# The opening of an attention-and-MLP kernel: four input tiles loaded in halves by two queues, the first keys through a third, two loads of v held back

## The chip, the cores and the metric

The kernel runs on one core of one Trainium2 chip. The metric is the device time of one execution in microseconds (us). The core has five engines that matter here: TensorE (PE in the profile, its weight loads PEld), VectorE (DVE), ScalarE (ACT), GpSimd (POOL) and SyncE (SP). SP, ACT and POOL can each put transfers on a DMA queue of their own. All three queues feed the same 16 DMA engines.

## The reference, cut to what matters

The input x has 2048 rows of 576 values. It is normalised row by row, and two branches work on the result: a sliding-window attention with 32 query heads and 16 key/value heads over the last 512 cached positions, and a gated MLP. All inputs are bf16.

```python
xn = layernorm(x)                                   # 1 x 2048 x 576
q = heads(xn @ wq)                                  # 32 heads of 128
k, v = k_cache[:, :, 1536:], v_cache[:, :, 1536:]   # 16 heads x 512 x 128, each used by 2 query heads
s = merge(softmax(q @ k.T * 128 ** -0.5) @ v) @ wo
h = gelu(layernorm(xn) @ w1)                        # four column groups, shifted by 1, -1, 2, -2 rows
x1 = xn + shifted(h) @ w2
g = silu(x1 + gelu(layernorm(x1) @ w3) @ w4)
out = x + s * g
```

## The kernel before, in words

**Tiling.** The rows of x are worked on in four blocks of 512 (NB = 4), each of four tiles of 128 rows (TB = 4, P = 128). The attention runs over "heads in blocks", u = 0 to 127, 32 for each block. For each u, PE multiplies the block by the head's part of wq (`stage_q`, or L729 for the first two), then takes the scores against the transposed keys kT (`stage_s`, L566), ACT takes the exponential (L569), and PE multiplies by v (`stage_v`, L588). The MLP follows. From about 9 us on, PE is the engine on which everything ends.

**The opening.** Before the first head can start, block 0 of x has to be loaded, normalised and transposed. Its four tiles live in `xn_b[0]`, seen as `x_first`. Tile 0 is loaded in two column halves, one by ACT's queue (L380) and one by SP's (L381). Tiles 1 and 2 are then loaded whole by SP's queue, and tile 3 whole by ACT's queue (all L384). Behind them SP's queue has, in an order written out by hand, the first two heads of keys (`load_k(0, nc.sync, 2, 0, 2)`, 256 KB, L364), then the first quarter of wq in two column halves (L393, L395), the other two heads of keys, v, more of wq, and so on.

`ln1_first` normalises the block. For tiles 0, 1 and 2, DVE takes the statistics (L431, L432), one tile after the other. Tile 3 goes to ACT, which takes its sum and its sum of squares (L435, L436). ACT also takes the square roots: one for tile 0 as soon as its statistics are there (L434), one for tiles 1 to 3 together (L440). DVE takes the reciprocals (L446 for tile 0, L448 for the others) and applies the result to tiles 0, 1 and 2 (L443); the first 256 columns of tile 3 are applied by ACT (L451) and the others by DVE (L454). The operations stand on each engine in the order in which they are written, and the engines wait for each other through semaphores.

PE meanwhile multiplies the identity 48 times (`warm`, L708), then waits for tile 2's statistics (`warm_behind`, L711) and multiplies five times more. Then it transposes: `tr1_first(pss, (0,))` makes five transposes of tile 0 (L470), `keys_first(0, k01)` four transposes of the first head of keys (L484), then come tile 1 (five), tiles 2 and 3 (ten), and `keys_first(1, k01)` with four more of keys. `xT_first` copies the transposed x out of PSUM (DVE three chunks, L478; ACT two, L476), DVE copies the two heads of keys to `kT` (L723), and PE starts the products for heads 0 and 1 (L729).

**POOL's queue.** POOL builds the identity, fills a few areas with constants (L387, L388, L402) and then puts loads on its queue. At step u = 3 of the head loop stands `load_v(2)`, two loads of 128 KB (v for key heads 4 and 5, L370), and behind it `load_wq(2)` (L345), which waits until PE has used the buffer that it overwrites. POOL has nothing to wait for ahead of `load_v(2)`.

`late(ap, fn)` makes POOL copy one element of `ap` to a scratch word (`gate`, L243) and then issue what `fn` issues, so that the transfers do not start before `ap` has been written.

**Near the end of the kernel,** `load_sx(b)` (L1048) loads, for block b, the attention result from DRAM and x again, through SP's queue; blocks 0 and 1 in one load for each of the two, blocks 2 and 3 in two halves.

Of the kernel before, what the change touches and what calls it, by code (L numbers as in the profile page):

```python
# [8 lines left out]
P = 128  # L9
# [22 lines left out]
def kernel(  # L32
# [14 lines left out]
    nc = tc.nc  # L47
# [15 lines left out]
    NB = S // QB  # L63
    TB = QB // P
# [18 lines left out]
    x2 = A_x.rearrange("b s d -> (b s) d")  # L83
# [158 lines left out]
    def late(ap, fn):  # L242
        g = nc.gpsimd.tensor_copy(out=gate[:, :], in_=ap)  # L243
        with tc.issue_after(g.ins):
            fn()
# [8 lines left out]
    def stage(i):  # L254
        return stage_pool.tile([P, DP * TB], BF16, name=f"stage{i % 2}")
# [43 lines left out]
    with ExitStack() as actx:  # L299
# [31 lines left out]
        x_t = {}  # L331
# [27 lines left out]
        def load_k(i, eng=None, step=4, g0=0, g1=4):  # L359
            if g0 == 0:  # L360
                kst_t[i] = stage(i)
            dst = kst_t[i][:, 0:4 * W].rearrange("p (g a) -> p g a", g=4)
            for g in range(g0, g1, step):
                (eng or nc.gpsimd).dma_start(  # L364
                    out=dst[:, g:g + step, :],
                    in_=A_k_cache[0, 4 * i + g:4 * i + g + step, K0:, :].rearrange("g (p kc) d -> p g (kc d)", p=P))

        def load_v(i, eng=None):
            for g in (2 * i, 2 * i + 1):
                (eng or nc.gpsimd).dma_start(out=v_sb[:, g, :, 0:Dh],  # L370
                                             in_=A_v_cache[0, g, K0:, :].rearrange("(p kc) d -> p kc d", p=P))
# [6 lines left out]
        x_first = xn_b[0][:, :, 0:D]  # L378
        hw = D // 2
        nc.scalar.dma_start(out=x_first[:, 0, hw:D], in_=x2[0:P, hw:D])  # L380
        nc.sync.dma_start(out=x_first[:, 0, 0:hw], in_=x2[0:P, 0:hw])  # L381
        for tt in range(TB):
            if tt:
                (nc.sync if tt < TB - 1 else nc.scalar).dma_start(out=x_first[:, tt, :],  # L384
                                                                  in_=x2[tt * P:(tt + 1) * P, :])
            x_t[0].append(x_first[:, tt, :])
        nc.gpsimd.memset(xn_b[0][:, :, D:], 0.0)  # L387
        nc.gpsimd.memset(wr_first[DR:, :], 0.0)  # L388
        with tc.manual_schedule(engines={SP}):
            load_k(0, nc.sync, 2, 0, 2)  # L390
            for m0 in (0, 2 * Dh):
                cols = slice(m0, m0 + 2 * Dh)
                nc.sync.dma_start(out=wq_b[0][:, :, cols],  # L393
                                  in_=A_wq[0:NF * P, cols].rearrange("(kc p) m -> p kc m", p=P))
                nc.sync.dma_start(out=wr_first[0:DR, cols], in_=A_wq[NF * P:D, cols])  # L395
            load_k(0, nc.sync, 2, 2, 4)
            load_v(0, nc.sync)
            load_wq(1, nc.sync)
            load_wr(1, 2, nc.sync)
            load_v(1, nc.sync)  # L400
            load_k(1, nc.sync)
# [7 lines left out]
        xn_t = {}  # L409
# [51 lines left out]
        def x_banks():  # L461
            a, b = (ps_sc.tile([P, 4, QB], BF16, name="ps_x", tag=f"sc{i}") for i in range(2))
            c, d = (ps_po.tile([P, 2, W], BF16, name="ps_x4", tag="po") for _ in range(2))
            return [c[:, 0, :], d[:, 0, :], a[:, 0, :], b[:, 0, :], b[:, 1, :]], a[:, 2:4, :]
# [15 lines left out]
        def keys_first(g, ps):  # L480
            src = kst_t[0]
            for kc in range(KCH):
                c0 = g * W + kc * P
                nc.tensor.transpose(out=ps[:, g, kc * P:(kc + 1) * P], in_=src[:, c0:c0 + P], identity=ident[:, :])  # L484
# [140 lines left out]
        def at(u, fn):  # L625
            fill.setdefault(u, []).append(fn)
# [64 lines left out]
        at(12, lambda: load_k(3))  # L691
        for g in range(Hkv):
            if g % 2 == 0 and g >= 4:
                at(max(2 * g - 8, 3), lambda g=g: load_v(g // 2))
        for j in range(2, NB * 8):
            at(4 * (j - 1) - 1, lambda j=j: load_wq(j))
        for i, u in enumerate((17, 21, 25, 28, 30, 33, 37, 41)):
# [4 lines left out]
        with tc.manual_schedule(engines={SP, POOL, PE, DVE, ACTE}):  # L702
            mv, nb = ln1_first()
            wu = ps_sc.tile([P, QB], FP32, name="warm", tag="sc0")

            def warm(n):
                for _ in range(n):
                    nc.tensor.matmul(wu[:, 0:112], lhsT=ident[:, :], rhs=ident[:, 0:112], start=True, stop=True)  # L708

            def warm_behind(ap):  # L710
                nc.tensor.matmul(wu[:, 0:1], lhsT=ident[:, :], rhs=ap.bitcast(BF16)[:, 1:2], start=True, stop=True)  # L711

            warm(48)
            warm_behind(mv[:, 2, :])
            warm(5)
            pss, k01 = x_banks()
            tr1_first(pss, (0,))
            keys_first(0, k01)
            tr1_first(pss, (1,))
            tr1_first(pss, (2, 3))  # L720
            keys_first(1, k01)
            xT_first(pss)
            nc.vector.tensor_copy(out=kT[:, 0:2, :], in_=k01[:, :, :])  # L723
            e = small.tile([P, 1], FP32, name="nr_e")
            nc.scalar.activation(out=e[:], in_=nb[:], func=ACT.Exp, scale=0.0)
            psq = [ps_pq.tile([P, QB], FP32, name="psq", tag="pq") for _ in range(2)]
            for u, kcs in ((0, (0,)), (1, (0,)), (0, range(1, NDC)), (1, range(1, NDC))):
                for kc in kcs:
                    nc.tensor.matmul(psq[u][:, :], lhsT=wq_main(u, kc), rhs=xT_b[0][:, kc, :],  # L729
                                     start=(kc == 0), stop=(kc == NDC - 1))  # L730
                if NDC - 1 in kcs:
                    qT_t[u] = qT_pool.tile([P, QB], BF16, name="qT")
                    nc.vector.tensor_copy(out=qT_t[u][:, :], in_=psq[u][:, :])
        turn, done = {}, 0
        for u in range(0, U + 1):
            n = 1
            if u in tr_k_at:
                n = 0
            if 12 < u < ln1_at[0] + 3 or u > WO_AT[1] + TB:
                n = 2  # L740
            n = min(n, OT + Hq * sum(u > v + TB for v in WO_AT.values()) - done)
# [6 lines left out]
        with tc.manual_schedule(engines={SP, POOL, PE}):  # L748
            for u in range(0, max(max(fill), max(pe_fill)) + 1):
                atoms = pe_fill.get(u, [])  # L750
                n = len(atoms)
# [44 lines left out]
    with ExitStack() as bctx:  # L796
# [144 lines left out]
        with tc.manual_schedule(engines={SP, POOL, PE, DVE, ACTE}):  # L941
# [6 lines left out]
            for half in range(2):  # L948
                nc.gpsimd.dma_start(out=w1_q[HALVES[half], :, :],
                                    in_=w1_tail.rearrange("p (g s) -> p g s", g=4)[:, :, P:c4])  # L950
# [18 lines left out]
            for k in range(len(ops) + 1):  # L969
                nxt = None  # L970
                if k < len(ops):
                    f, b, p = ops[k]
# [3 lines left out]
                if pend:  # L976
# [3 lines left out]
                    f, b, p = ops[k - 1]  # L980
# [61 lines left out]
        def load_sx(b):  # L1042
            s_b = sx_pool.tile([P, TB, D], BF16, name="s_b")
            x_b = sx_pool.tile([P, TB, D], BF16, name="x_b")
            n = TB if b < 2 else TB // 2
            for t, src in ((s_b, s_dram), (x_b, x2)):
                for t0 in range(0, TB, n):
                    nc.sync.dma_start(out=t[:, t0:t0 + n, :], in_=rows(src, b * TB + t0, n))  # L1048
            sx_t[b] = (s_b, x_b)
# [150 lines left out]
        with tc.manual_schedule(engines={PE, DVE, ACTE}):  # L1200
# [6 lines left out]
            g, j = 2, 0  # L1207
            for d in range(0, ND, 2):
                b = d // NP
# [56 lines left out]
            b = NB - 1  # L1266
# [15 lines left out]
        with tc.manual_schedule(engines={PE, DVE, ACTE, SP}):  # L1282
# [20 lines left out]
            tt = TB - 1  # L1303
# [22 lines left out]
    with tc.If(flag > 0):  # L1326
        nc.gpsimd.dma_start(out=g_dram[(NT - 1) * P:NT * P, :], in_=g_last)
        with ExitStack() as gctx:
# [20 lines left out]
            with tc.For_i(0, NT, 1) as t:  # L1349
# [10 lines left out]
                with tc.For_i(0, Hq, 1) as h:  # L1360
                    g = h // REP
# [6 lines left out]
                                        in_=A_wq[0:NF * P, cols].rearrange("(kc p) m -> p kc m", p=P))  # L1368
# [72 lines left out]
```

## Time and profile before

| | |
|---|---|
| time, median of three runs | 813.63 us (813.28 to 818.35) |
| time of the profiled execution | 814.01 us |
| span of the profiled execution | 812.2 us |
| PE busy | 806.3 us (99%) |
| DVE busy | 464.7 us (57%) |
| ACT busy | 402.2 us (50%) |
| POOL busy | 95.8 us (12%) |
| granted TensorE clock | 1.0 |

The profile is one execution taken by the hardware profiler. The span runs from the first to the last recorded instruction; the execution's own time of 814.01 us is 1.8 us longer. Times in a timeline count from the start of the span. A row of a timeline gives the start, the time for which the group ran, the engine, the line of the kernel, the operation, what it writes and reads, how many there are (x5), and in brackets how long the engine had been idle before it and what released it. The chain of waits is followed backwards from the last instruction, at each step to what released it, so it shows which work set the end. A DMA row gives the issuing queue, the size and the time from issue to landing.

### The profile page before, as it was taken

Reading aid. Unit: us, or ns where it says so; the run is one execution under the profiler, and the core shown is the slowest. Engines: PE = TensorE matmul, PEld = TensorE weight load, DVE = VectorE, ACT = ScalarE, POOL = GpSimd, SP = SyncE. Lnnn points to the kernel's source line nnn. Section 1 sums busy time; section 2 is a strip of 40 time slices with the busy share of each in tenths; the row PEclk is TensorE's granted clock in tenths of the full one; section 3 lists DMA queues with packets and bytes.
Section 4 is the critical chain, followed back from the end, with each engine's and each line's share of the span. In section 5 each row is a group of like instructions: output and inputs, shape, how many; then the busy total and the mean of one; then the engine's idle time right before and its main releaser. Section 6 shows DMA issues by size and latency. Waiting matters only on the chain.

```text
span 812.2 us, 19806 instructions
## 1 busy us (share of the span) xinstructions
PE 806.3 (99%) x8231; PEld 471.1 (58%) x8231; DVE 464.7 (57%) x1398; ACT 402.2 (50%) x503; POOL 95.8 (12%) x162
## 2 busy tenths in 40 slices
PE   8999999999999999999999999999999999999998
PEld 6666666566655666655666556555555555555555
DVE  5978786228963379752477539353246636655413
ACT  7777777237762377742577542033343333334621
POOL 3333210100010000000100301362000000000000
PEclk9999999999999999999999999999999999999999
DMA  9999881109760187520373372499000410220101
GB/s 218 203 168 222 187 173 57 56 27 141 156 151 9 56 137 139 111 53 27 103 126 76 84 93 61 100 324 255 3 2 16 92 45 16 49 89 17 46 15 39
DMA packets 137437, 80.00 MB, mean 99 GB/s; under 512 B 114784, under 2 KB 128384, under 8 KB 137344
## 3 DMA queue, kind: packets, MB, share of 16 engines
q1 hardware_dynamic: 124656, 40.03, 27.5%
q0 software_dynamic: 11296, 37.27, 16.8%
q8 instruction: 65, 1.06, 0.6%
q10 hardware_dynamic: 1392, 1.40, 0.5%
q14 instruction: 28, 0.23, 0.1%
HBM read 45.38 MB, written 6.93 MB: 64 GB/s over the span
## 4 chain that ended last, share of the span: by engine, by line
PE 99%; DMA 0%; DVE 0%; SPq 0%; issue 0%; ACT 0%
PE ph L1077 15%; PE po L588 15%; PE sc L566 14%; PE psq L548 13%; PE sc L269 12%; PE pm L1114 12%; PE pm L1289 4%; PE pm L1077 3%; PE pm L832 2%; PE pswo L269 2%; PE pr L1114 2%; PE ph L832 1%; PE sc L523 1%; PE pr L269 1%; PE pm L269 1%; PE pr L879 1%
## 5 line engine op out<-in xcount | busy, mean ns | idle before, releaser
L569 ACT ACTIVATE pT<-sc 128x1024 bf16<-128x1024 f32 x256 | 250.5, 1023 | 129.5 <-PE sc L566 129.2
L588 PEld LDWEIGHTS <-pT 128*128 128x128 bf16 x2048 | 133.1, 98 | 54.4 <-issue 5.1
L588 PE MATMUL po<-v_sb,pT 128*128 128x129 bf16 x2048 | 154.7, 220 | 0.0
L566 PE MATMUL sc<-qT,kT 128*128 128x512 bf16 x512 | 152.1, 379 | 0.0
L548 PE MATMUL psq<-xT_b,wq_b 128*128 128x512 bf16 x503 | 129.1, 379 | 0.0
L1077 PE MATMUL ph<-xT_b,w_s 64*128 64x512 bf16 x976 | 127.4, 376 | 0.0
L1114 PE MATMUL pm<-w_s,h 64*128 64x512 bf16 x864 | 122.2, 377 | 0.0
L1095 ACT ACTIVATE h<-ph 128x512 bf16<-128x512 f32 x67 | 39.4, 598 | 132.6 <-PE ph L1077 130.4
L269 PE MATMUL sc<-wo_sb,oT 128*128 128x512 bf16 (+1 forms) x768 | 103.9, 286 | 0.0
L1114 PEld LDWEIGHTS <-h 64*128 64x128 bf16 x1728 | 71.0, 94 | 55.0
L269 PEld LDWEIGHTS <-oT 128*128 128x128 bf16 x1024 | 65.2, 98 | 55.2 <-issue 0.5
L592 DVE RECIPROCAL ri_b<-po 128x2 f32<-128x2 f32 x256 | 40.4, 164 | 97.7 <-PE po L588 88.5
L593 DVE TENSOR_TENSOR o<-po,ri_b 128x256 bf16<-128x256 f32 x216 | 89.7, 422 | 4.9
L1114 PE MATMUL pr<-w_s,h 64*128 64x64 bf16 x864 | 90.3, 189 | 0.0
L1077 PEld LDWEIGHTS <-w_s 64*128 64x128 bf16 x1152 | 56.1, 94 | 48.2 <-issue 0.6
L556 DVE TENSOR_TENSOR qT<-psq,rq 128x512 bf16<-128x512 f32 x82 | 56.6, 691 | 35.5 <-PE psq L548 35.1
L1093 DVE COPY hx<-ph 128x512 f32<-128x512 f32 x55 | 38.1, 692 | 60.4 <-PE ph L1077 60.4
L548 PEld LDWEIGHTS <-wq_b 128*128 128x128 bf16 x503 | 46.3, 98 | 42.6
L566 PEld LDWEIGHTS <-kT 128*128 128x128 bf16 x512 | 44.4, 98 | 28.4 <-issue 0.2
L345 POOL DMA_DIRECT2D wq_b<-in_A_wq_dram x30 | 22.6, 754 | 285.1 <-PE psq L548 256.2
L558 DVE CAST qT<-psq 128x512 bf16<-128x512 f32 x44 | 30.2, 686 | 23.2 <-PE psq L523 21.0
L807 DVE TENSOR_SCALAR hx<-ph,ph 1x1 f32<-1x1 f32 x55 | 11.5, 210 | 46.4 <-PE ph L1077 46.4
(178 smaller groups left out, 727.7 us busy)
## 6 DMA issues: line engine op xcount, KB each, us to landing
wq_b<-in_A_wq_dram POOLq DMA_DIRECT2D x30, 512.0 KB, 4.8
wo_sb<-in_A_wo_dram POOLq DMA_DIRECT2D x8, 576.0 KB, 4.7
w_s<-in_B_w_dram POOLq DMA_DIRECT2D x9, 512.0 KB, 6.3
w_s<-in_B_w_dram POOLq DMA_DIRECT2D x10, 288.0 KB, 5.4
w_s<-in_B_w_dram POOLq DMA_DIRECT2D x4, 576.0 KB, 6.1
out_dram<-o SPq DMA_DIRECT2D x15, 144.0 KB, 1.8
oT<-o SPq DMA_TRANSPOSE x108, 3.3
xn_b<-in_A_x_dram POOLq DMA_DIRECT2D x12, 144.0 KB, 2.8
```

The costliest lines, as they stand in the source:

```text
L269: nc.tensor.matmul(ps, lhsT=oT_t[qb * Hq + h][:, tt, :], rhs=wo_sb[:, h, lo:hi], start=(i == 0), stop=(i == Hq - 1))
L548: nc.tensor.matmul(psq[:, :], lhsT=wq_main(u, kc), rhs=xT_b[qb % 2][:, kc, :], start=(kc == 0 and pos != 1), stop=(kc == n - 1 and (plain ...
L556: behind["qT"] = nc.vector.tensor_tensor(out=qT[:, :], in0=psq[:, :], in1=rq_t.pop(u), op=ALU.add)
L566: nc.tensor.matmul(sc[:, j, :], lhsT=kT[:, g, kc * P:(kc + 1) * P], rhs=qT_t[u][:, :], start=True, stop=True)
L569: nc.scalar.activation(out=pT[:], in_=sc[:], func=ACT.Exp, scale=SCALE)
L588: nc.tensor.matmul(po[:, j, :], lhsT=pTs[kc][:, tt * P:(tt + 1) * P], rhs=v_sb[:, g, kc, 0:Dh + 1], start=(kc == 0), stop=(kc == KCH - 1))
L592: nc.vector.reciprocal(out=ri, in_=po[:, :, Dh])
L593: nc.vector.tensor_tensor(out=o[:, t0:t0 + 2, :], in0=po[:, :, 0:Dh], in1=ri.unsqueeze(2).to_broadcast([P, 2, Dh]), op=ALU.mult)
L1077: nc.tensor.matmul(ps[i][:, :], lhsT=lhsT, rhs=xT[half, kc, :], start=first, stop=last, skip_group_check=True)
L1093: nc.vector.tensor_copy(out=src[:, :], in_=ps[i][:, :])
L1095: nc.scalar.activation(out=h3[:, :], in_=src[:, :], func=ACT.Gelu_apprx_tanh)
L1114: nc.tensor.matmul(out, lhsT=h3_t[b, fc][half, tt * P:(tt + 1) * P], rhs=w4_s[fc // WS][half, fc % WS, lo:hi], start=key not in started, s ...
```

## The change

Five things are changed.

1. Tiles 1, 2 and 3 of x's first block are no longer loaded whole. Each is loaded in two halves of 64 rows, the upper rows by SP's queue and the lower by ACT's, in the order 1, 3, 2.
2. The first two heads of keys go through POOL's queue; they stood on SP's queue behind x. They are issued outside the part of the program whose order is fixed by hand.
3. PE's transposes of the first head of keys move from behind tile 0 to behind tiles 2 and 3, where those of the second head were.
4. `load_v(2)` at step u = 3 stands behind a `late` gate on the first element of tile 0 of the normalised x.
5. `load_sx(2)` loads block 2 whole; only block 3 is still in halves.

```diff
-        for tt in range(TB):
-            if tt:
-                (nc.sync if tt < TB - 1 else nc.scalar).dma_start(out=x_first[:, tt, :],
-                                                                  in_=x2[tt * P:(tt + 1) * P, :])
-            x_t[0].append(x_first[:, tt, :])
+        for tt in (1, TB - 1, 2):
+            for eng, half in ((nc.scalar, 1), (nc.sync, 0)):
+                r0 = half * P // 2
+                eng.dma_start(out=x_first[r0:r0 + P // 2, tt, :], in_=x2[tt * P + r0:tt * P + r0 + P // 2, :])
+        x_t[0] = [x_first[:, tt, :] for tt in range(TB)]
         nc.gpsimd.memset(xn_b[0][:, :, D:], 0.0)
         nc.gpsimd.memset(wr_first[DR:, :], 0.0)
+        load_k(0, nc.gpsimd, 2, 0, 2)
         with tc.manual_schedule(engines={SP}):
-            load_k(0, nc.sync, 2, 0, 2)
             for m0 in (0, 2 * Dh):
...
-                at(max(2 * g - 8, 3), lambda g=g: load_v(g // 2))
+                at(max(2 * g - 8, 3), lambda g=g: load_v(g // 2) if g > 4 else
+                   late(xn_t[0][0:1, 0, 0:1], lambda: load_v(2)))
...
             tr1_first(pss, (0,))
-            keys_first(0, k01)
             tr1_first(pss, (1,))
             tr1_first(pss, (2, 3))
-            keys_first(1, k01)
+            for g in range(2):
+                keys_first(g, k01)
             xT_first(pss)
...
-            n = TB if b < 2 else TB // 2
+            n = TB if b < NB - 1 else TB // 2
```

## The prediction

> **What bounds the kernel now.** I read the page first: the busy times and the chain of waits over the whole span.
>
> ```profile
> span 812.2 us, 19806 instructions
> ...
> PE 806.3 (99%) x8231; PEld 471.1 (58%) x8231; DVE 464.7 (57%) x1398; ACT 402.2 (50%) x503; POOL 95.8 (12%) x162
> ...
> PE 99%; DMA 0%; DVE 0%; SPq 0%; issue 0%; ACT 0%
> PE ph L1077 15%; PE po L588 15%; PE sc L566 14%; PE psq L548 13%; PE sc L269 12%; PE pm L1114 12%; PE pm L1289 4%; PE pm L1077 3%; PE pm L832 2%; PE pswo L269 2%; PE pr L1114 2%; PE ph L832 1%; PE sc L523 1%; PE pr L269 1%; PE pm L269 1%; PE pr L879 1%
> ```
>
> PE is the chain for 99% of 812.2 us, and nothing in the change takes a multiplication away. So the change can only move the time at which PE begins its unbroken work. I therefore read the chain of waits of the first 16 us.
>
> ```profile
> 1.44 3.37 DMA xn_b<-in_A_x_dram
> ...
> 4.83 0.83 DVE ln_st L431 x2
> ...
> 9.10 0.22 PE ps_x L484 x4
> 9.32 2.19 PE psq L729 x10
> ```
>
> The opening is a load (until 4.81), DVE work on it, and PE's transposes; from 9.3 us the chain stays on PE. All that can be won lies ahead of 9.3 us. The timeline of this stretch, in order of time, carries all terms below.
>
> ```profile
> 0.98 0.40 ACTq L380 DMA_DIRECT2D xn_b<-in_A_x_dram  x1
> 1.42 0.47 ACTq L384 DMA_DIRECT2D xn_b<-in_A_x_dram  x1
> 1.44 0.91 SPq L384 DMA_DIRECT2D xn_b<-in_A_x_dram  x2
> ...
> 1.87 4.66 PE L708 MATMUL warm<-ident 128*128 128x112 bf16 x48 [1.87 <-POOL ident masks.py:199]
> ...
> 1.92 1.28 ACT L426 ACT_TABLE_LOAD   x1 [1.92 <-PEq L1425]
> 2.39 0.43 SPq L364 DMA_DIRECT2D stage<-in_A_k_cache_dram  x1
> ...
> 2.92 1.63 POOL L370 DMA_DIRECT2D v_sb<-in_A_v_cache_dram  x2
> ...
> 3.24 0.82 DVE L431 BATCH_NORM_STATS2 ln_st<-xn_b 128x6 f32<-128x288 bf16 x2 [2.13 <-DMA xn_b<-in_A_x_dram]
> ...
> 4.40 0.30 ACT L434 ACTIVATE nr_y<-ln_mv,eps_t 128x1 f32<-128x1 f32 x1 [0.98 <-DVE ln_mv L432]
> ...
> 4.83 0.82 DVE L431 BATCH_NORM_STATS2 ln_st<-xn_b 128x6 f32<-128x288 bf16 x2 [0.53 <-DMA xn_b<-in_A_x_dram]
> 5.03 0.69 ACT L435 ACTIVATE wo_sb<-xn_b 128x576 f32<-128x576 bf16 x1 [0.33 <-DMA xn_b<-in_A_x_dram]
> ...
> 5.82 0.77 DVE L431 BATCH_NORM_STATS2 ln_st<-xn_b 128x6 f32<-128x288 bf16 x2
> ...
> 6.86 0.30 ACT L440 ACTIVATE nr_y<-ln_mv,eps_t 128x3 f32<-128x3 f32 x1
> ...
> 6.89 0.43 DVE L443 TENSOR_SCALAR xn_b<-xn_b,ln_mv,nr_y 128x576 bf16<-128x576 bf16 x1
> ...
> 7.44 0.77 DVE L443 TENSOR_SCALAR xn_b<-xn_b,ln_mv,nr_y 128x576 bf16<-128x576 bf16 x2
> ...
> 7.66 0.39 PE L484 MATMUL ps_x<-ident,stage 128*128 128x128 bf16 x4
> 7.76 0.60 ACT L451 ACTIVATE xn_b<-xn_b,nr_m,nr_y 128x256 bf16<-128x256 bf16 x1
> ...
> 7.92 1.17 PE L470 MATMUL ps_x<-ident,xn_b 128*128 128x128 bf16 x15
> ...
> 8.69 1.09 DVE L478 COPY xT_b<-ps_x 128x512 bf16<-128x512 bf16 x3 [0.21 <-PE ps_x L470]
> ...
> 8.93 0.39 PE L484 MATMUL ps_x<-ident,stage 128*128 128x128 bf16 x4
> ...
> 9.17 1.26 PE L729 MATMUL psq<-xT_b,wq_b 128*128 128x512 bf16 x5
> ```
>
> Two rows wait for x: DVE 0.53 us for tile 1 (4.83) and ACT 0.33 us for tile 3 (5.03). Tile 2 is not waited for. The last thing that a transpose of tile 3 needs from ACT is L451, which ends at 7.76 + 0.60 = 8.36. The last four transposes of keys start at 8.93, and the first product at 9.17. Four keys thus take 0.24 us of PE's queue. The first four, at 7.66, lie in a time in which PE waits for DVE's apply of tile 1 (from 7.44; its transposes start at 7.92): they are free there.
>
> **The change, part by part.** The transfers are priced by their landings and by the rate of the DMA engines.
>
> ```profile
> xn_b<-in_A_x_dram ACTq DMA_DIRECT2D x1, 144.0 KB, 3.6
> xn_b<-in_A_x_dram SPq DMA_DIRECT2D x1, 144.0 KB, 3.4
> xn_b<-in_A_x_dram SPq DMA_DIRECT2D x1, 72.0 KB, 2.2
> xn_b<-in_A_x_dram ACTq DMA_DIRECT2D x1, 72.0 KB, 2.4
> ...
> stage<-in_A_k_cache_dram SPq DMA_DIRECT2D x1, 256.0 KB, 4.9
> wq_b<-in_A_wq_dram SPq DMA_DIRECT2D x1, 256.0 KB, 5.4
> v_sb<-in_A_v_cache_dram POOLq DMA_DIRECT2D x1, 128.0 KB, 5.2
> ...
> DMA to landing us min/median/max: 4.8/5.3/7.3
> ...
> 3.00:4.00 1.00, 1.00 (x14) 1.00 (x13) 0.76 (x2) 0.41 (x2) 1.00 (x2) 1.00 0.91 298
> ```
>
> (The row of `stage` is keys on SP's queue. The row that begins with DMA is the spread over v's loads up to 25 us. The last row is the window from 3 to 4 us, with the busy times of the engines, then the granted clock, the busy share of the DMA engines, 0.91, and their rate, 298 GB/s.)
>
> *Tiles 1, 3, 2 in halves.* Tile 0 has landed at 0.98 + 2.4 = 3.38 at the latest. At 298 GB/s a tile of 144 KB passes in 0.49 us, so in their order tile 1 lands at about 3.87, tile 3 at 4.37, tile 2 at 4.86. Bounds: no sooner than 1.42 + 2.2 = 3.6 for tile 1; and, if a half is as slow as a whole tile today, tile 1 at 1.44 + 3.4 = 4.84, tile 3 (issued one issue of 0.47 later) at 1.89 + 3.6 = 5.49. I take the first values: the two rows of 72 KB are the same size and queues, and today's tiles 1 and 3 share the engines. On ACT, three half loads replace one whole, two issues more, 0.94 us: the table load goes from 1.92 to about 2.86 and ends at 4.14; a square root of at most 0.30 us behind it ends at 4.44, against the 4.40 at which L434 starts. At most 0.04 us, taken as nothing; the cover is ACT's 0.98 us of idle time.
>
> *DVE then.* A tile of statistics takes 5.82 - 4.83 = 0.99 us. Tile 1 starts at 3.24 + 0.99 = 4.23 instead of 4.83, tile 2 at 5.22, the apply of tile 0 at 6.29 instead of 6.89. That is 0.60 us, but it isn't what sets the end.
>
> *ACT then.* L435 cannot start before L434 ends, 4.40 + 0.30 = 4.70, so about 4.72 instead of 5.03: 0.31 us. The rest of ACT's chain follows: L440 ends at 6.85 instead of 7.16, the applies of tiles 1 and 2 start at 7.13, L451 ends at 8.05 instead of 8.36. So what is late next is ACT: of DVE's 0.60 us only 0.31 counts. The 48 warming multiplications still end at 1.87 + 4.66 = 6.53, and tile 0's transposes may slip by some tenths behind them: tile 1's cannot start before 7.92 - 0.31 = 7.61.
>
> *Keys behind the tiles.* The keys' transposes can start at 8.93 - 0.31 = 8.62. There are eight now, not four: 2 x 0.24 = 0.48 us. The first product starts at 9.10 instead of 9.17: of 0.31 us, 0.24 are given back, because the first four keys leave the free place. DVE's copies of x (8.69, now 8.38; three in 1.09) and kT's copy stay ahead of their users.
>
> *Keys through POOL's queue.* They need to be there at 8.62 instead of 7.66. The trace has no such load this early. They take the place that v's pair has on that queue, 2.92 (sooner if they go ahead of the last fill). By the row of the same bytes on SP's queue, 4.9 us, they land at 7.8; by v's first row, 5.2 us, at 8.1; by v's slowest, 7.3 us, at 10.2. I take 8.1, the nearest row by queue and time, half a microsecond early. On SP's queue their issue of 0.43 us goes and one more half tile comes: wq is issued at about the same 2.85, and by its 5.4 us lands at 8.3, ahead of 9.10.
>
> *v's two loads behind tile 0.* The gate is a one-element copy and its wait ends with the apply of tile 0, about 6.7 us. Behind it on POOL's queue stands wq's load:
>
> ```profile
> 16.46 0.75 POOL L345 DMA_DIRECT2D wq_b<-in_A_wq_dram  x1 [11.91 <-PE psq L548]
> ```
>
> POOL idles 11.91 us there, so the gate and the two issues (1.63 us) cost nothing; were that idle time gone, they'd push wq's second quarter by their 1.6 us and the wait. The bytes land at about 6.7 + 0.8 + 5.3 = 13, at worst 15. Head 8 is the first that uses them: the three attention products hold 42% of 812 us for 128 heads, 2.7 us a head, so about 11.4 + 8 x 2.7 = 33 us. Hidden.
>
> *load_sx(2).* Two SP issues fewer, around 716 us:
>
> ```profile
> L1048 SPq DMA_DIRECT2D s_b<-s_dram x6: 377/462/2637, 555.4 to 717.2; - x6
> ```
>
> SP isn't in the chain there; nothing (between 0 and 2 x 0.46 us of SP's own time).
>
> **Sum.** PE starts 0.07 us sooner, and since the chain is PE from there to the end, the whole time moves by that: 814.01 - 0.07 = 813.94 for the profiled execution. That execution is 0.38 above the median of 813.63, so the median goes to 813.56. Bounds from above: -0.31 if the eight keys cost PE nothing, +1.5 if keys land at 10.2.
>
> **A rule against it.** The row of 3 to 4 us shows the DMA engines already at 91% with 298 GB/s, whatever queue feeds them. The Trainium skill (DMA: Bandwidth & Descriptors, Rules for kernel authors) says of two transfers to disjoint halves of the partitions "Don't bother — they serialize", since both run over the same 16 engines, and that spreading over queues doesn't raise the bandwidth. By that rule the halves bring nothing in themselves, and if nothing else moved either, the sum would be that of rival (a) below, +0.24 us. I hold that the order (tile 1 no longer sharing with tile 3) brings the gain, which the rule doesn't deny; no run yet shows which.
>
> **Rivals.**
> (a) *The halves land no sooner.* Tile 1 at 4.84 and ACT's start at 5.03 as today. Then only the eight keys count: the first product at 9.17 + 0.24 = 9.41, 813.9 in the median; with tile 3 at 5.49 it is 0.46 more, 814.3. For it: the engines are saturated. Against it: the 72 KB rows, 2.2 and 2.4 us.
> (b) *Slower: keys late.* POOL's queue delivers the keys after 8.62 and PE, which takes its instructions in order, stands at L484. From a landing at 8.69 on, the gain is gone; halfway from 8.6 to the 10.2 bound, at 9.4, it is +0.7, 814.3; at the bound +1.5, 815.2. For it: v's slowest load and DMA engines that stay full. Against it: v's pair leaves the same queue. It would reach 1% only with a landing near 16.7 us, which no row comes near.
> (c) *More is kept.* ACT's 0.31 us comes through whole, because PE takes the keys while it would wait for x's copies anyway: 813.3. Against it: first product and last key are 9.17 and 8.93, back to back today.
>
> **How the numbers follow.** Forecast 0.56, (a) 0.15, (b) 0.20, (c) 0.06, something unnamed 0.03. The predicted time is 813.6. For the range I add the spread of the two near runs before (813.28 and 813.63, 0.35) to (c) below, 812.9, and to the middle of (b) and the end of (a), with some more of (b), above, 814.9. What a measurement of this kernel can tell from no change is about 1%, 8.1 us; no case reaches that: faster 0.01, same 0.97, slower 0.02, the latter for a wait that I don't see.
>
> **What would show it.** In the changed profile: L431 of tile 1 at 4.2 with hardly any idle time before it; L435 at 4.7, right behind L434; L451 ending near 8.05; eight L484 in one row from 8.6 without a wait for a DMA; L729 at 9.1; everything after it as before. If L484 waits for the keys, (b) holds; if L431 still idles half a microsecond for tile 1, (a). The prediction is wrong if L729 starts outside 8.8 to 10.3, or if the time after it changes by more than a few tenths.

## The result, and the profile after

| | before | changed |
|---|---|---|
| time, median of six runs each | 813.8 us (813.28 to 818.35) | 818.57 us (818.32 to 820.92) |
| ratio, with its 95% interval | | 1.0057 [1.0034, 1.0079] |
| profiled execution / its span | 814.01 / 812.2 us | 818.32 / 816.6 us |

The changed kernel is 4.8 us slower by the medians, and the predicted range ended at 814.9. (A ratio is a mean over rounds, so single executions some us above the others are in it; they move a median little.)

From the changed kernel's page, the span, the busy times, and the shares of the chain of waits:

```profile
span 816.6 us, 19734 instructions
...
PE 804.2 (98%) x8150; PEld 470.8 (58%) x8231; DVE 464.9 (57%) x1398; ACT 402.1 (49%) x503; POOL 96.6 (12%) x164
...
PE 94%; SPq 2%; DMA 1%; issue 1%; DVE 1%; ACT 0%; DVEq 0%; ACTq 0%
```

No engine has much more to do than before, POOL 0.8 us (81 of PE's multiplications have no record in this trace, so its busy time is a little short). The chain of waits has left PE for 6% of the span, which was 1%. In the opening it is a poor guide, since it runs over a load of later keys that lands at 10.07, 0.04 us after the work for which PE's transposes wait. The changed kernel's timeline shows better where PE waits (its lines after 385 stand one higher than before: the products are L730, the transposes of keys still L484):

```profile
1.44 1.83 ACTq L385 DMA_DIRECT2D xn_b<-in_A_x_dram  x3
1.44 2.11 SPq L385 DMA_DIRECT2D xn_b<-in_A_x_dram  x3
...
2.33 0.84 POOL L364 DMA_DIRECT2D stage<-in_A_k_cache_dram  x1
...
3.29 1.28 ACT L426 ACT_TABLE_LOAD   x1 [3.29 <-issue]
...
4.74 0.82 DVE L431 BATCH_NORM_STATS2 ln_st<-xn_b 128x6 f32<-128x288 bf16 x2 [0.47 <-DMA xn_b<-in_A_x_dram]
...
4.82 0.29 ACT L434 ACTIVATE nr_y<-ln_mv,eps_t 128x1 f32<-128x1 f32 x1
...
6.53 0.68 ACT L435 ACTIVATE wo_sb<-xn_b 128x576 f32<-128x576 bf16 x1 [1.42 <-DMA xn_b<-in_A_x_dram]
...
7.41 0.82 DVE L431 BATCH_NORM_STATS2 ln_st<-xn_b 128x6 f32<-128x288 bf16 x2 [1.61 <-DMA xn_b<-in_A_x_dram]
...
8.53 0.16 PE L712 MATMUL warm<-ln_mv,ident 128*128 128x1 bf16 x1 [2.00 <-DVE nr_y L446]
...
9.41 0.60 ACT L451 ACTIVATE xn_b<-xn_b,nr_m,nr_y 128x256 bf16<-128x256 bf16 x1
...
11.12 1.06 PE L484 MATMUL ps_x<-ident,stage 128*128 128x128 bf16 x8
...
11.97 0.63 PE L730 MATMUL psq<-xT_b,wq_b 128*128 128x512 bf16 x1
...
14.93 1.02 PE L566 MATMUL sc<-qT,kT 128*128 128x512 bf16 x4
```

The rows to compare are those quoted in the prediction. Tile 1's statistics start at 4.74 (before 4.83), hardly sooner. Tile 3 on ACT starts at 6.53 instead of 5.03, tile 2 at 7.41 instead of 5.82, and both now wait for a DMA, 1.42 and 1.61 us. PE stands idle for 2.00 us behind its 48 warming multiplications, before the late ones. The first product starts at 11.97 instead of 9.17, the first scores at 14.93 instead of 11.43.

The last halves are late in two ways. The six halves take longer to issue than three tiles did: three on ACT's queue 1.83 us (0.61 each), three on SP's 2.11 (0.70 each), where whole tiles took 0.47 and 0.46 each. And from issue to landing they take longer than tile 0's halves do; the changed kernel's DMA view for the issues up to 4 us:

```profile
xn_b<-in_A_x_dram SPq DMA_DIRECT2D x4, 72.0 KB, 3.8
xn_b<-in_A_x_dram ACTq DMA_DIRECT2D x4, 72.0 KB, 2.9
stage<-in_A_k_cache_dram POOLq DMA_DIRECT2D x1, 256.0 KB, 4.5
```

3.8 and 2.9 us in the median of tile 0's half and the three new ones, where tile 0's halves took 2.2 and 2.4 before. One by one, tile 1's halves land at 4.47 and 4.64, tile 3's at 4.82 and 6.45, tile 2's at 7.08 and 7.32. The keys on POOL's queue, issued at 2.33, land at 6.88, before both halves of tile 2, which were issued behind them. Tile 3's late half is the one whose issue on SP's queue runs from 2.07 to 2.89, past the start of the keys' issue. The changed kernel's DMA view of 4 to 5 us shows both on the engines at once:

```profile
DMA packets 68, 0.12 MB, mean 121 GB/s; under 512 B 9, under 2 KB 50, under 8 KB 68
...
q1 hardware_dynamic: 43, 0.04, 51.2%
q0 software_dynamic: 18, 0.07, 31.7%
```

q0 is the queue that POOL fills: 0.07 of the 0.12 MB are its. In two more executions of the changed kernel (experiments 13 and 14) it has 0.14 of 0.20 and 0.20 of 0.27 MB of that microsecond; before, it had nothing of the 0.24. So the keys take most of these bytes. The low rate of 121 GB/s is this execution's own: the other two show 204 and 266, and before it was 240.

The second loss is the clock. The third value from the right (behind POOL's) in the changed kernel's windows is the granted clock:

```profile
8.00:10.00 2.00, 1.31 (x16) 0.83 (x15) 1.89 (x8) 1.59 (x6) 0.97 (x3) 1.00 1.18 276
10.00:12.00 2.00, 1.95 (x20) 1.93 (x20) 1.04 (x4) 0.86 (x3) 0.65 (x1) 0.50 1.11 308
12.00:14.00 2.00, 1.78 (x8) 0.79 (x8) 1.02 (x2) 1.72 (x3) 0.00 (x0) 0.65 1.18 215
```

From 10.0 to 13.4 us PE runs at half its clock, right as it starts its work; the eight L484 above take 1.06 us. Before, it was 1.0 from 6.75 us to the end of PE's work. The record begins only there (here at 6.59), and the 1.0 that windows give for earlier times, and the table of before for the whole span, says nothing of what lies ahead of it: the warming multiplications ahead of the record's beginning start 93 ns apart, and those behind it 49 (experiment 4 shows both in one row). So in both kernels PE warms up at half the clock until then.

Three smaller steps come later, found by setting the starts of the same weight loads of two kernels against each other: 0.17 us near 87 us, 0.26 at 235 us, 0.5 at 486 us. With the 3.50 us at the first scores they make 4.4, the difference of the spans (816.6 - 812.2).

### The profile page after: what moved, and what is told of

The parts are those of the page before. It is cut to its first block, busy times and chain, and to the rows that moved or that the text cites. A ratio compares the mean times of both kernels' runs of the same rounds, so it can differ in the third digit from the quotient of the medians.

```text
span 816.6 us, 19734 instructions
## 1 busy us (share of the span) xinstructions
PE 804.2 (98%) x8150; PEld 470.8 (58%) x8231; DVE 464.9 (57%) x1398; ACT 402.1 (49%) x503; POOL 96.6 (12%) x164
## 3 DMA queue, kind: packets, MB, share of 16 engines
q8 instruction: 65, 1.06, 0.6%
## 4 chain that ended last, share of the span: by engine, by line
PE 94%; SPq 2%; DMA 1%; issue 1%; DVE 1%; ACT 0%; DVEq 0%; ACTq 0%
PE ph L1078 15%; PE po L588 14%; PE sc L566 13%; PE psq L548 13%; PE sc L269 12%; PE pm L1115 11%; PE pm L1290 4%; PE pm L1078 3%; PE pm L833 2%; SPq L260 2%; PE pr L1115 2%; PE sc L523 1%; PE pr L269 1%; PE ph L833 1%; PE pm L269 1%
## 5 line engine op out<-in xcount | busy, mean ns | idle before, releaser
L566 PE MATMUL sc<-qT,kT 128*128 128x512 bf16 x504 | 150.4, 379 | 0.0
L548 PE MATMUL psq<-xT_b,wq_b 128*128 128x512 bf16 x452 | 123.5, 379 | 2.8
L269 PE MATMUL sc<-wo_sb,oT 128*128 128x512 bf16 (+1 forms) x756 | 101.8, 284 | 0.8
```

Source lines behind the costliest of these rows:

```text
L269: nc.tensor.matmul(ps, lhsT=oT_t[qb * Hq + h][:, tt, :], rhs=wo_sb[:, h, lo:hi], start=(i == 0), stop=(i == Hq - 1))
L548: nc.tensor.matmul(psq[:, :], lhsT=wq_main(u, kc), rhs=xT_b[qb % 2][:, kc, :], start=(kc == 0 and pos != 1), stop=(kc == n - 1 and (plain ...
L566: nc.tensor.matmul(sc[:, j, :], lhsT=kT[:, g, kc * P:(kc + 1) * P], rhs=qT_t[u][:, :], start=True, stop=True)
```

## The experiments

The theories, with the letters that the expectations use: that keys on POOL's queue hold up x by themselves (Q); that the halves do by themselves (H); that it takes both (I); that it is the cut into rows (R); and that the halved clock is a loss of its own (C). Times are medians, set against the kernel before in the same call.

**Experiment 1: the changed kernel, with the first keys back on SP's queue.**

```diff
-        load_k(0, nc.gpsimd, 2, 0, 2)
         with tc.manual_schedule(engines={SP}):
+            load_k(0, nc.sync, 2, 0, 2)
```

> The changed kernel with one thing undone: the first two heads of keys are again on SyncE's queue, behind x. Theory Q (the keys on GpSimd's queue are served beside the halves of x and delay tiles 3 and 2): tile 3 is there by about 5.0 us instead of 6.5, the first product starts at 9.4, and the time is back to 814 to 814.5 us. Theory H (the row halves themselves, six issues on two queues, are slow to land): tile 3 is still there only after 6.0 us, the first product starts at 11 to 12, and the time stays at 817 to 818.6 us.

815.74 us against 813.52, ratio 1.0037 [1.0021, 1.0053]. From its timeline:

```profile
5.03 0.68 ACT L435 ACTIVATE wo_sb<-xn_b 128x576 f32<-128x576 bf16 x1
...
5.87 0.82 DVE L431 BATCH_NORM_STATS2 ln_st<-xn_b 128x6 f32<-128x288 bf16 x2 [0.21 <-DMA xn_b<-in_A_x_dram]
...
9.70 1.27 PE L730 MATMUL psq<-xT_b,wq_b 128*128 128x512 bf16 x5
```

Between the two expectations. Without a load on POOL's queue (v's pair is held back here until 7.61) the halves come about as whole tiles did, and not sooner: from issue to landing the three new ones of each queue take 2.7 to 3.05 us, and whole tiles, of twice the bytes, 2.85 to 3.1 (experiment 11). What is issued later lands later: tile 2 is complete at 5.78, whole at 4.91. L435 has no wait here; it stands right behind L434, which starts at 4.82 because ACT's issues come first. The first product is 0.5 us later than in the profile before, and 0.8 later than in experiment 11.

**Experiment 2: the kernel before, with only the halves in rows.**

> The kernel before with one thing done: tiles 1, 3 and 2 in row halves by both queues, in that order; keys and v as before. Theory Q: tile 3 lands between 4.4 and 5.0 us and the time is 813.3 to 814 us. Theory H: tile 3 lands after 6 us, PE's clock drops, and the time is 816.5 to 818.5 us.

817.12 us, ratio 1.0037 [1.0026, 1.0049]. Its seven runs fall into two groups, 814.92 to 815.65 with a mean clock of 0.999 to 1.0, and 817.12 to 817.43 with 0.997 to 0.998. The profiled one is of the first group: tile 3 at 5.77, tile 2 at 6.41, first product at 9.84. So Q fails: the halves cost time with the keys on SP's queue as well (v's loads leave POOL's queue at 2.91 here).

**Experiment 3: the kernel before, with only the keys on POOL's queue.**

> The kernel before with one thing done: the first two heads of keys on GpSimd's queue; x whole, v's loads as before. Theory Q: x's last tile lands about 1 us later than before (6 us), and the time is 815 to 816.5 us. Theory H: x lands as before by 5.1 us, and the time is 813.5 to 814.3 us.

813.83 us, ratio 1.0013 [0.9995, 1.0031]; tile 3 starts at 4.64, and the first product at 9.01, between the 9.17 of before's profile and the 8.88 of its second one (experiment 11). Keys on POOL's queue do no harm to whole tiles.

**Experiment 4: the changed kernel with 70 warming multiplications instead of 48.**

```diff
-            warm(48)
+            warm(70)
```

> The changed kernel with 70 instead of 48 warming multiplications, so that PE has work until about 8.6 us. Theory C (2 us of idle PE bring its granted clock to 0.5 from 10.0 to 13.4 us, and this is a part of the loss of its own): the clock stays at 1.0, the first product starts at about 10.9 instead of 11.97, the first scores at 13.3 instead of 14.93, and the time falls by 1.3 to 1.7 us to about 817 us. Rival (only the late x counts): the time stays at 818.5 us.

816.6 us, ratio 1.0038 [1.0024, 1.0052]. From its windows, and behind them its timeline:

```profile
10.00:12.00 2.00, 1.95 (x26) 1.51 (x26) 1.72 (x6) 1.25 (x3) 0.97 (x2) 1.00 0.86 244
12.00:14.00 2.00, 2.00 (x11) 0.84 (x9) 1.52 (x4) 1.66 (x3) 0.00 (x0) 1.00 1.09 260
```

```profile
6.36 0.68 ACT L435 ACTIVATE wo_sb<-xn_b 128x576 f32<-128x576 bf16 x1 [1.25 <-DMA xn_b<-in_A_x_dram]
...
7.73 0.82 DVE L431 BATCH_NORM_STATS2 ln_st<-xn_b 128x6 f32<-128x288 bf16 x2 [1.96 <-DMA xn_b<-in_A_x_dram]
...
8.85 0.16 PE L712 MATMUL warm<-ln_mv,ident 128*128 128x1 bf16 x1 [1.90 <-DVE nr_y L446]
...
11.44 1.27 PE L730 MATMUL psq<-xT_b,wq_b 128*128 128x512 bf16 x5
...
13.71 1.02 PE L566 MATMUL sc<-qT,kT 128*128 128x512 bf16 x4
```

x is as late as in the changed kernel, the clock stays at 1.0, and the first scores start at 13.71 instead of 14.93. So the halved clock is a loss of its own: 1.2 us at that point, 2.0 by the medians (818.57 - 816.6), the rest being steps of the later path that this kernel lacks (those at 87 and 486 us). The 70 multiplications end at 6.94, not near the expected 8.6, since from 5.0 us on they start 49 ns apart. The idle time ahead of L712 is thus still 1.90 us, so it isn't the length of this one gap that decides on the clock; what does is taken up below.

**Experiment 5: the changed kernel with column halves instead of row halves.**

```diff
-                r0 = half * P // 2
-                eng.dma_start(out=x_first[r0:r0 + P // 2, tt, :], ...)
+                cs = slice(half * hw, (half + 1) * hw)
+                eng.dma_start(out=x_first[:, tt, cs], in_=x2[tt * P:(tt + 1) * P, cs])
```

> The changed kernel with the halves of tiles 1, 3 and 2 cut by columns (128 rows of 288 values, as tile 0's) and not by rows (64 rows of 576). Theory R (a half of 64 rows is dear to issue, 0.58 to 0.82 us where tile 0's column halves take 0.40 to 0.42): the issues take 0.40 to 0.47 each, the last half is issued by 2.4 instead of 2.94, tile 2 is there by 6.0 instead of 7.4, and the time is 814 to 815.5 us. Theory N (it is the number of issues on two queues at once, whatever their shape): the issues take 0.6 us and more, tile 2 lands after 7 us, and the time stays at 817 to 819 us.

815.09 us, ratio 1.0023 [1.0013, 1.0033]. From its timeline:

```profile
1.42 1.44 ACTq L385 DMA_DIRECT2D xn_b<-in_A_x_dram  x3
1.44 1.38 SPq L385 DMA_DIRECT2D xn_b<-in_A_x_dram  x3
...
4.31 0.77 DVE L431 BATCH_NORM_STATS2 ln_st<-xn_b 128x6 f32<-128x288 bf16 x2
...
5.92 0.68 ACT L435 ACTIVATE wo_sb<-xn_b 128x576 f32<-128x576 bf16 x1 [1.13 <-DMA xn_b<-in_A_x_dram]
...
6.18 0.82 DVE L431 BATCH_NORM_STATS2 ln_st<-xn_b 128x6 f32<-128x288 bf16 x2 [0.86 <-DMA xn_b<-in_A_x_dram]
```

A column half is issued in 0.48 and 0.46 us, as a whole tile is. Tile 1 then comes in time for DVE, but tiles 3 and 2 are still waited for. (The clock was 0.5 from 8.3 to 11.7 us in this profiled execution of 816.75 us.) R holds for the issues and for a part of the time only.

**Experiment 6: the changed kernel with the tiles loaded whole, as before.**

> The changed kernel with the halves alone undone: tiles 1, 2 and 3 whole and on the queues of the kernel before; keys on GpSimd's queue, their transposes behind the tiles, the gate on v and the whole load near the end stay. Theory I (the halves' later issue puts the keys ahead of the last halves on the engines; whole tiles are issued before the keys and are not delayed): tile 3 is there by 4.7, the first product starts between 9.0 and 9.3, the time is 813.3 to 814.2 us. Theory K (the keys on GpSimd's queue cost the opening together with the gate or the order of the transposes): first product after 10 us, 815 us or more.

814.1 us, ratio 1.0023 [1.0007, 1.0039]; the profiled span is 812.2 us, as before. From its timeline:

```profile
4.68 0.67 ACT L435 ACTIVATE wo_sb<-xn_b 128x576 f32<-128x576 bf16 x1
...
7.33 0.60 ACT L451 ACTIVATE xn_b<-xn_b,nr_m,nr_y 128x256 bf16<-128x256 bf16 x1
...
8.54 0.61 PE L484 MATMUL ps_x<-ident,stage 128*128 128x128 bf16 x8
...
8.99 1.27 PE L730 MATMUL psq<-xT_b,wq_b 128*128 128x512 bf16 x5
```

The changed kernel without its halves has lost little (0.6 us by the medians, 0.07% at the least by the interval, nothing in the profiled span), though the keys leave POOL's queue at 2.33 here too. The 4.8 us take the halves and a load beside them: I holds.

**Experiment 7: experiment 3 with the gate on v as well.**

> The kernel before with the first keys on GpSimd's queue and v's two loads behind the gate, nothing else: x whole, transposes of keys where they were. If v's loads compete with x or the keys, the first product starts a little sooner than with the keys alone (9.01) and the time is 813.2 to 813.6 us; if the gate costs anything later it shows as a wait for v near head 8, about 33 us, and the time is above 814 us.

813.86 us, ratio 1.0015 [0.9995, 1.0035]; first product at 8.90. The time lies between the two expectations; against experiment 3 the gate costs nothing.

**Experiment 8: the kernel before with 30 warming multiplications instead of 48.** Here x comes as before, so that the clock is the main suspect.

> The kernel before with 30 instead of 48 warming multiplications, so that PE is idle from about 4.7 to 6.9 us; x, keys and v as before. Theory C (some 2 us of idle PE cost its clock): the granted clock is 0.5 for about 3.4 us behind 8 us, the first scores start 1 to 2 us later than 11.43, and the time rises by as much, to 814.8 to 815.8 us. Rival (idle PE at this place costs nothing): the time stays at 813.3 to 814 us.

815.0 us (813.3 to 816.15), ratio 1.0009 [0.9994, 1.0025], which settles nothing by itself: three of its ten executions are at 813.3 to 813.8, as before, and seven at 814.7 to 816.15. In the profiled execution (815.65 us) PE idles 1.53 us, the clock is 0.5 from 8.2 to 11.6 us, and the first scores start at 13.14; part of that is a wait of 0.63 us for keys, which PE reaches sooner here.

**Experiment 9: experiment 2 with 70 warming multiplications.**

> The kernel before with the row halves (as in the run with the halves alone) and 70 warming multiplications, so that PE is not idle for long. It separates the late landing from the clock. If the runs of the halves alone fall into two groups, 814.9 to 815.7 and 817.1 to 817.4 us, because the clock falls in some of them, all runs lie at 814.3 to 815.7 us here, and none at 817. If the second group has another cause, it is here too.

816.28 us (815.47 to 816.87) against 813.87, ratio 1.0031 [1.002, 1.0042], with a mean clock of 0.999 to 1.0 in all seven runs. No run is at 817 any more, as C said, but six of the seven lie above the expected 815.7, by up to 1.2 us; why is open. Tile 3 starts at 5.67, tile 2 at 6.66, the first product at 10.06.

**Experiment 10: experiment 4 with the keys' load held back until tile 1 has landed.**

```diff
-        load_k(0, nc.gpsimd, 2, 0, 2)
+        late(x_first[0:1, 1, 0:1], lambda: load_k(0, nc.gpsimd, 2, 0, 2))
```

> The changed kernel with 70 warming multiplications and the first keys' load on GpSimd's queue behind a gate on tile 1 of x, so that its bytes cannot run beside the last halves. To be compared with the changed kernel with 70 warming multiplications (816.6 us, tile 3 at 6.36, tile 2 at 7.73, first product at 11.44). Theory I (the keys overtake the last halves): tile 3 is there by 5.4 and tile 2 by 6.2; the keys land near 9 to 9.5 and PE may wait for them; first product at 9.5 to 10.2, time 814.2 to 815.3 us. Rival (it is not the keys' bytes but the order in which the halves are issued): tile 2 still after 7 us and 816 us or more.

815.76 us, ratio 1.0027 [1.0016, 1.0038]. From its timeline:

```profile
4.84 0.84 POOL L364 DMA_DIRECT2D stage<-in_A_k_cache_dram  x1
5.30 0.68 ACT L435 ACTIVATE wo_sb<-xn_b 128x576 f32<-128x576 bf16 x1 [0.19 <-DMA xn_b<-in_A_x_dram]
...
6.05 0.82 DVE L431 BATCH_NORM_STATS2 ln_st<-xn_b 128x6 f32<-128x288 bf16 x2 [0.22 <-DMA xn_b<-in_A_x_dram]
...
10.08 0.62 PE L484 MATMUL ps_x<-ident,stage 128*128 128x128 bf16 x8 [0.54 <-DMA stage<-in_A_k_cache_dram]
```

Only the time of the keys' load differs from experiment 4, and tile 3 comes 1.06 us sooner, tile 2 1.68, as theory I has it. Now the keys are late instead, at 10.03, and PE waits 0.54 us for them. So the first product starts at 10.54, a little behind the expected 10.2, and the time is 0.5 us above the expected range.

**Experiment 11: the kernel before, once more.** No edit; are the waits of 0.53 and 0.33 us, which the change was to remove, always there?

> The kernel before, unchanged, profiled once more. In the profiled execution shown, 814.01 us, DVE waits 0.53 us for tile 1 and ACT 0.33 us for tile 3. If that wait belongs to the kernel, it is here again, within 0.1 us. If it was that execution's own (the others' median is 813.5 us), tile 1 starts at 4.3 without a wait, the first product before 8.8, and the span is 811.7 us.

813.92 us, span 812.1. From its timeline:

```profile
4.55 0.82 DVE L431 BATCH_NORM_STATS2 ln_st<-xn_b 128x6 f32<-128x288 bf16 x2
4.73 0.67 ACT L435 ACTIVATE wo_sb<-xn_b 128x576 f32<-128x576 bf16 x1
...
7.48 0.60 ACT L451 ACTIVATE xn_b<-xn_b,nr_m,nr_y 128x256 bf16<-128x256 bf16 x1
...
8.88 1.26 PE L729 MATMUL psq<-xT_b,wq_b 128*128 128x512 bf16 x4
```

Neither row has a wait. The two waits belonged to one execution. Without them the first product starts 0.29 us sooner, and the whole time is still within 0.1 us of the profile before.

**Experiment 12: the kernel before with only the column halves.**

> The kernel before with tiles 1, 3 and 2 in column halves by both queues, in that order; keys on SyncE's queue, v as before. If halving in that order can pay at all, it does so here, where an issue is shortest and no load of keys runs beside it: tile 1 at 4.2, tile 3 by 4.6, 813.0 to 813.5 us. If more issues only mean a later last tile, tile 2 is there after 5.6 us and the time is 813.8 to 815 us.

815.24 us, ratio 1.002 [1.0011, 1.0029], outside both expectations. Tile 1 starts at 4.35 without a wait, tile 3 at 5.01 after 0.19, tile 2 at 5.33, so the tiles come about as early as whole ones; but the first keys are awaited for 0.40 us at 7.98, and the first product starts at 9.28, 0.4 later than in experiment 11. The steps at 235 and 486 us are most of the rest of the loss.

**Experiments 13 and 14: the changed kernel, twice more.** No edit.

> The changed kernel, unchanged, profiled again. If the loss of the clock belongs to every run: PE idle for about 2 us between 6 and 8.5 us, the granted clock 0.5 for 3.41 us, the first scores at 14.5 to 15.2 us. If it is the landing alone that varies: clock 1.0, tile 2 of x after 8 us.

> The changed kernel, unchanged, profiled a third time, for the scatter of the landings: tile 3 between 6.2 and 6.8, tile 2 between 7.2 and 7.9 us if the late landing belongs to the change; the clock as in the run before this.

818.9 and 818.34 us. Tile 3 starts at 6.45 and 6.35, tile 2 at 7.30 and 7.48: the loss repeats, unlike the waits of before, and so do the three later steps. In experiment 14 the clock is 0.5 from 9.7 to 13.1 us. In experiment 13 its record begins only at 14.5 us and the mean is 1.0, although all its warming multiplications start 93 ns apart and its eight L484 take 1.06 us: it had half the clock until then. A mean of 1.0 is thus no proof of a full clock.

**Experiment 15: the kernel before, with only tile 3 cut, in three column parts on ACT's queue.**

```diff
+        for c in range(0, D, D // 3):
+            nc.scalar.dma_start(out=x_first[:, TB - 1, c:c + D // 3],
+                                in_=x2[(TB - 1) * P:TB * P, c:c + D // 3])
```

> The kernel before with tile 3 of x loaded in three column parts by ScalarE's queue, two issues more on that queue and none on SyncE's. If the step of 0.25 us near 235 us goes with the number of ScalarE's instructions, it is there; if it goes with the halves on both queues or with a late opening, PE runs through that place as in the kernel before.

817.79 us in its one run, against 814.04. From its timeline:

```profile
6.21 0.68 ACT L435 ACTIVATE wo_sb<-xn_b 128x576 f32<-128x576 bf16 x1 [1.41 <-DMA xn_b<-in_A_x_dram]
```

The two uncut tiles keep their places (4.33 and 5.40); the cut one lands 1.5 us later than whole (6.21 against 4.73). The clock halves here too. The step at 235 us is there.

## Why the prediction was wrong

**The step that failed** is "Tiles 1, 3, 2 in halves". It said that "in their order tile 1 lands at about 3.87, tile 3 at 4.37, tile 2 at 4.86", with 4.84 and 5.49 as the worst for tiles 1 and 3, and "I take the first values". Tile 1 was there at 4.6, tile 3 at 6.45 and tile 2 at 7.3. The step divided bytes by the rate of a full microsecond, as if the six pieces stood in one row and nothing else ran. But a half takes as long from issue to landing as a whole tile (experiment 1), so its landing follows its issue; the step left out that each of the six has to be issued (the last at 2.94, the last whole tile at 1.93), and what runs beside the late ones by then. Most profiles line up by that, x's pieces and what POOL's queue had put out before 5 us:

| kernel | pieces of x | first load on POOL's queue | tile 3 starts | tile 2 starts |
|---|---|---|---|---|
| 11 (before again) | whole | v, 2.92 | 4.73 | 5.53 |
| 6 | whole | keys, 2.33 | 4.68 | 5.33 |
| 3 | whole | keys, 2.33 | 4.64 | 5.65 |
| 12 | columns | v, 2.92 | 5.01 | 5.33 |
| 5 | columns | keys, 2.33 | 5.92 | 6.18 |
| 15 | tile 3 in three columns | v, 2.91 | 6.21 | 5.40 |
| 1 | rows | none (v, 7.61) | 5.03 | 5.87 |
| 10 | rows | keys, 4.84 | 5.30 | 6.05 |
| 2 | rows | v, 2.91 | 5.77 | 6.41 |
| 9 | rows | v, 2.91 | 5.67 | 6.66 |
| 4 | rows | keys, 2.33 | 6.36 | 7.73 |
| changed | rows | keys, 2.33 | 6.53 | 7.41 |

With whole tiles, a load on POOL's queue at 2.33 doesn't touch x. With row halves, the sooner it goes out, the later the last tiles: experiment 10 against 4 changes only that. (The sooner loads are the bigger ones too; the two weren't tried apart.) That POOL's load holds up the halves issued beside and behind it is shown; how the engines share their time between queues isn't. It needn't be POOL's queue: in experiment 15 the third part of tile 3 is issued at 2.37, beside the keys on SP's queue at 2.40, and is the late one, with v on POOL's queue as in 12. What the smaller rows of the pieces (576 and 384 bytes in columns) add in experiments 5, 12 and 15 wasn't tried by itself.

By this step the first scores stand at 13.71 (experiment 4), 2.3 us late, of which some 0.26 are the keys' (below). A smaller miss of the same kind lies on ACT: its two more issues were to take 0.94 us, with L434 at most 0.04 late. The table load starts at 3.29 instead of 1.92, 1.37 later, and L434 at 4.82 instead of 4.40. The wait for tile 3 covers it here. In experiment 1, where that wait is gone, L435 starts at 5.03 right behind L434, just where it started before, so this term alone would have taken the 0.31 us that ACT was to gain.

**What the sum lacked: the clock.** The prediction kept the warming multiplications where they were and asked only whether the transposes slip behind them. With x late, PE idles between the two, and 3.4 us of half a clock follow: 1.2 us at the first scores. The Trainium skill (TensorE: Matmul & The Clock Gate, Part 1, What's actually happening) says that the clock is halved after at least one idle window of about 3.4 us, and that the window runs freely. The trace agrees on the length (0.5 for 3.41 us) and on the free run, but not on the threshold. The record changes only at steps of 3.41 us from its beginning, and it begins anywhere from 4.7 to 7.4 us (14.5 in experiment 13). So a gap counts by how much of it lies in one step. In the first step behind the record's beginning PE is idle for 2.31 us (experiment 14), 2.23 (8), 2.09 (the changed kernel), 1.70 (15) and 1.61 (5), and the half clock follows; with 1.70 (2), 1.47 (4), 1.29 (1) and less in the others it doesn't. In experiment 4 the step at 8.41 cuts the gap of 1.90 us in two. From 1.6 to 1.7 us both happen, and what decides there is open.

**The base.** The gain was to come from the waits of 0.53 and 0.33 us. In experiment 11 there are none, nor in 6, 7 and 8, which have whole tiles too; in 3 DVE waits 0.33 us and ACT not at all. The landing of x moves by some tenths from one execution to the next; there was nothing steady to win.

**The steps after the opening.** "The whole time moves by that" was right for the opening; three steps came on top. At 235 us ACT's three exponentials in a row take 3.10 us instead of 2.85 (the changed kernel, then the kernel before):

```profile
235.34 3.10 ACT L569 ACTIVATE pT<-sc 128x1024 bf16<-128x1024 f32 x3 [0.70 <-PE sc L566]
```

```profile
231.67 2.85 ACT L569 ACTIVATE pT<-sc 128x1024 bf16<-128x1024 f32 x3 [0.69 <-PE sc L566]
```

All kernels with two more issues on ACT's queue have this step, experiment 15 too, which has none more on SP's; 3, 6, 7, 8 and 11 don't. So it goes with ACT's added instructions; by what way is open. At 486 us PE waits for `hs`, DVE waits ahead of it for the transfer `hq`, and that one stands on SP's queue behind eight transposes L260 (the changed kernel's waits of 479 to 495 us, its timeline, and that of experiment 11):

```profile
DVE hs L908 <- DMA hq<-h: 1.3, 1, 1.3
PEld L833 <- DVE hs L908: 0.5, 1, 0.5
```

```profile
469.94 13.36 SPq L260 DMA_TRANSPOSE xnnT<-xm_b  x8
```

```profile
465.73 12.37 SPq L260 DMA_TRANSPOSE xnnT<-xm_b  x8
```

The eight took 13.0 to 13.8 us in the changed kernel's three executions and in 5, 9, 10, 12 and 15, and 11.7 to 12.9 in all the others. DVE's wait for `hq` was 1.0 to 1.4 us where PE was held up (the changed kernel, 5, 12 and 15), and 0.4 and 0.6 in 9 and 10, where it wasn't; so the length of the eight doesn't settle it alone. Why they differ, and what the step at 87 us is (0.15 to 0.38 us), which only the changed kernel shows, stays open.

**What held.** Keys through POOL's queue: the landing was taken as 8.1 and was 6.88, and L484 has no wait, so rival (b) didn't come. Keys behind the tiles: 0.24 us were set for the four more; from the start of L451 to the first product it is 1.66 us in experiment 6 and 1.40 in experiment 11, so 0.26. The gate on v: nothing (experiment 7 against 3). load_sx(2): no step near 716 us. "What is late next is ACT" didn't hold: where the tiles come in time, in experiments 6 and 11, the chain of waits of the opening runs through DVE's statistics and apply to PE's transposes, with no row of ACT's, as it did in the profile before. In experiment 6 the first product lies 0.18 us ahead of the profile before in spite of the keys' 0.26, so some 0.44 came through and not 0.31.

**The rivals.** Rival (a) had the kind right, "the halves land no sooner", and the size wrong: 0.2 to 0.7 us for what was 2.3 and, with the clock and the later steps, 4.8. Its rule from the Trainium skill (DMA: Bandwidth & Descriptors, Rules for kernel authors), not to bother with two transfers to disjoint halves of the partitions, agrees with every kernel with row halves here, and the runs go further: the halves are a loss, 0.37% [0.26, 0.49] by themselves in experiment 2, the clock's part in four of its seven executions included. The prediction weighed that rule at 0.15 and against it put two rows of 72 KB, which were the first loads of all, on idle engines. Rival (c) needed ACT's 0.31 us, which the late x took away, and the keys' 0.26 aren't hidden in experiment 6 either.

No kernel was faster than the one before: experiments 3, 7 and 8 are level with it within their intervals.

## What to carry to other kernels

A load cut in pieces is not sooner there when a piece takes as long from issue to landing as the whole (2.7 to 3.05 us against 2.85 to 3.1 here): each piece costs its issue (0.4 to 0.8 us), the last one goes out later, and then loads of another queue go ahead of it. A wait of a few tenths on a DMA at the start should be seen in a second execution before a change is built on it. And whatever delays the first real work of PE can leave it idle behind its warm-up and cost the clock as well, so the two have to be moved together.

## What the runs showed of the hardware

- A row half (64 partitions, 72 KB) takes 0.61 to 0.70 us to issue in a row of three, a column half (128 partitions, 72 KB) and a whole tile (144 KB) 0.46 to 0.48.
- The granted clock changed only at steps of 3.41 us, whose place differed from execution to execution. PE idle for 1.6 to 2.3 us within one step was followed by a step at half the clock in five profiles; 1.47 us and less never were, and 1.70 went both ways.
- Ahead of the beginning of the clock's record, at 4.7 to 7.4 us (once 14.5), the warming multiplications start 93 ns apart, behind it 49.
- With no load on POOL's queue, a row half of 72 KB landed 2.7 to 3.05 us after its issue, a whole tile of 144 KB 2.85 to 3.1 (experiments 1 and 11).
- The same eight DMA transposes took 11.7 to 13.8 us in executions of nearly equal kernels; PE was held up behind them in six of the eight executions from 13.0 us on, and in none below.
